# Decode attention with a gated MLP on one core: the last projection chunks in two column tiles and two PSUM tiles, a one-chunk last load, and bias loads on SyncE's queue

## The chip, the core and the metric

The kernel runs on one core of one Trainium2 chip. The metric is the device time of one execution in microseconds; the median of several runs is given. Beside it stands one profiled execution, whose trace all views come from. TensorE is PE (its weight loads PEld), VectorE is DVE, ScalarE is ACT, GpSimd is POOL, SyncE is SP. All times are in microseconds from the start of the span unless another unit is named.

## The reference

Eight tokens (batch 8, one position each) of width 448 go through two branches, which a gate mixes.

```python
g = sigmoid((x * gate_w).sum(-1))
# A: attention of one query over the last W = 1024 positions of a cache
q = (x @ wq)                                  # 16 heads of 256, 8 key/value heads
scores = einsum("bhqd,bhkd->bhqk", q, k) * 256 ** -0.5
a = einsum("bhqk,bhkd->bhqd", softmax(scores), v).reshape(8, 1, 4096) @ wo
# B: layernorm, then an MLP with 1792 hidden units
b = gelu(layernorm(x) @ w1 + b1) @ w2 + b2
out = g * a + (1 - g) * b                     # 8 x 448
```

All tensors are bf16. For every token the kernel reads 4 MiB of keys and 4 MiB of values; with the weights that is 77.67 MB.

## The kernel before

**Loads.** All large loads go through a ring of four slots (`slot`, 4 MiB each) in the order of a plan: keys 0, wq, keys 1, values 0, keys 2, values 1, and so on to values 6, then w1 (with room for w2), values 7 with w2, and wo. They are all issued by SP (`nc.sync.dma_start`: L128 for keys and values, L140 for rows of weights, L157 for w2). A slot is loaded again once what read it is done (`done()`, `pump()`). Keys and values of a token are cut in two halves by key/value heads (`kv_loader`); `cuts` cuts the halves again: keys 0 has `(2, 1)`, its first half in two pieces of 1024 KB and its second half in one of 2048 KB. In the built program each transfer counts its landing on one of eight counters, taken in turn, and its issue waits for the landing of the transfer eight before it.

**Each token.** `transpose_keys(b)` turns the keys on TensorE (L360) and copies them out on ACT (L366) and DVE (L368); one group of sixteen goes by DVE and POOL (L330, L338). `scores(b)` multiplies with the queries (L427), `top` takes the maximum (L440), `expo` the exponential (L444), `turn`, `scale` and `bring` make the weights ready for `values(b)` (L498), and `finish` and `spread` (L511 to L524) put the sums of heads into `oP`, which is the stationary operand of the last projection. The order of all this is written out by hand; `steps(b)` places the softmax of one token between the transposes of the next.

**Biases.** `biases` issues the loads of b2 (one row) and b1 (four rows of 448, on partitions 0, 32, 64, 96) on ACT's queue, after the transposes of token 1 (`steps(0)`, place 15). `norm`, in the transposes of token 2 (place 14), spreads these rows over partitions on DVE (L307, L309) before the reduction of token 2's scores (L440).

**The last projection.** What is left at the end is 46 chunks, each a product of an 8-column stationary operand with 128 rows of 448 columns: 14 of the MLP (`hs` with w2), 32 of the attention (`oP` with wo). The wo load is cut by `cuts` into pieces of whole chunks, eight chunks to each of four quarters `q`: quarters 0 and 1 in one piece each, quarter 2 in two pieces of 4, quarter 3 in pieces of 2, 4 and 2 chunks. The first 40 chunks are `wide` (L632): chunk i goes to column tile i % 4 of TensorE and so to a 32-partition block of the PSUM tile A1. DVE adds b2 to A1 (`accs`, L639). The last `TAIL` = 6 chunks are `narrow` (L643): each is cut in four column blocks of 112, one per column tile, all in one PSUM tile A2. Between them, at place `TAIL - LATE` = 4, stands the product with `pick` (f32, L643), which adds up the four blocks of `accs`. Then DVE copies blocks 0 and 1 of A2 and ACT blocks 2 and 3 (L656), and each half is stored by SP and by ACT (L657).

Of the kernel before, what the change touches and what calls it, by code (L numbers as in the profile page):

```python
# [11 lines left out]
BF16 = mybir.dt.bfloat16  # L12
F32 = mybir.dt.float32
# [4 lines left out]
def kernel(  # L18
# [15 lines left out]
    nc = tc.nc  # L34
    P = nc.NUM_PARTITIONS

    NB, Sq, D = A_x.shape
# [8 lines left out]
    QD = 4  # L46
    BL = P // QD
# [13 lines left out]
    NCK = W // SK  # L61
    CB = 4
    UR = NG * rep
    HALF = D // 2
    DO = D // QD
    J8 = Dh // BL
    NQW = Hq // QD
    HS = NCK * Dh
    SLOT = NG * HS
    RING = 4  # L70
    TAIL = 6
    LATE = 2
    qscale = float(Dh) ** -0.5

    xf = A_x.rearrange("b s d -> (b s) d")
    out_f = out.rearrange("b s d -> (b s) d")

    ctx.enter_context(tc.manual_schedule())
    consts = ctx.enter_context(tc.tile_pool(name="consts", bufs=1))
# [6 lines left out]
    ps_kt = ctx.enter_context(tc.tile_pool(name="ps_kt", bufs=3, space=PSUM))  # L86
# [19 lines left out]
    def add(key, loader):  # L106
        index[key] = len(plan)
        plan.append(loader)

    def slot(*key):  # L110
        return slots[index[key]]

    def kv_loader(src, b, cuts=(1, 1), inner=False):
        pieces = [
            (i, k, cuts[i])
            for i in range(NG)
            for k in range(cuts[i])
        ]
        if inner:
            pieces.sort(key=lambda x: x[1])  # L120

        def load(t):
            for i, k, m in pieces:
                v = src[b, i * QD : (i + 1) * QD, kv_base:Sk, :].rearrange(
                    "a (s c) d -> s a (c d)", c=NCK
                )
                n = HS // m
                nc.sync.dma_start(  # L128
                    t[:, i * HS + k * n : i * HS + (k + 1) * n],
                    v[:, :, k * n : (k + 1) * n],  # L130
                )

        return load

    def rows_loader(pieces):
        def load(t):
            o = 0
            for ap in pieces:
                n = ap.shape[-1]
                nc.sync.dma_start(t[:, o : o + n], ap)  # L140
                o += n

        return load
# [12 lines left out]
        kv_loader(A_v_cache, NB - 1, (2, 2), True)(t)  # L156
        nc.sync.dma_start(slot("w12")[:, OW2 : OW2 + FB * D], w2_v)  # L157

    add(("k", 0), kv_loader(A_k_cache, 0, (2, 1)))
    add(("wq",), rows_loader(wq_r + [wq_t]))  # L160
    for b in range(1, NB):
        add(("k", b), kv_loader(A_k_cache, b))
# [4 lines left out]
        (NQW - 2, 0, 4),  # L167
        (NQW - 2, 4, 8),
        (NQW - 1, 0, 2),
        (NQW - 1, 2, 6),  # L170
        (NQW - 1, 6, 8),
    ]
    add(("wo",), rows_loader([wo_v[:, q, j0 * D : j1 * D] for q, j0, j1 in cuts]))

# [4 lines left out]
    b2_r = consts.tile([BL, D], BF16)  # L179
    b1_r = consts.tile([P, FQ], BF16)  # L180
# [1 line left out]
    nc.scalar.dma_start(g_r[0:1, :], gate_w.rearrange("(o d) -> o d", o=1))  # L182

    def biases():
        nc.scalar.dma_start(b2_r[0:1, :], B_b2.rearrange("(o d) -> o d", o=1))
        nc.scalar.dma_start(b1_r[::BL, :], B_b1.rearrange("(t d) -> t d", t=QD))

    ident = consts.tile([P, P], BF16)
    make_identity(nc, ident[:])
# [418 lines left out]
    b = NB - 1  # L608
# [10 lines left out]
    finish(b)  # L619
    spread(b)  # L620

    A2 = ps_kt.tile([P, DO], F32, tag="ktp", name="A2")
    w2 = slot("w12")
    w = slot("wo")
    NCH = NQW * J8
# [2 lines left out]
    ] + [(oP[:, c % J8, c // J8, :], w[:, c * D : (c + 1) * D]) for c in range(NCH)]  # L628
    wide, narrow = chunks[:-TAIL], chunks[-TAIL:]
    for i, (lhsT, rhs) in enumerate(wide):  # L630
# [4 lines left out]
            rhs=rhs,  # L635
# [3 lines left out]
    nc.vector.tensor_tensor(accs[:], A1[:], b2s[:], op=ALU.add)  # L639
    narrow.insert(TAIL - LATE, (pick[:], accs[:]))  # L640
    for i, (lhsT, rhs) in enumerate(narrow):
        for t in range(QD):
            nc.tensor.matmul(  # L643
                A2[BL * t : BL * t + NB, :],
                lhsT=lhsT,
                rhs=rhs[:, t * DO : (t + 1) * DO],
                start=(i == 0),
                stop=(i == TAIL),
            )
    for h, (eng, copy) in enumerate(  # L650
        ((nc.sync, nc.vector.tensor_copy), (nc.scalar, nc.scalar.copy))
    ):
        res = consts.tile([NB, 2, DO], BF16, name=f"res{h}")
        for i in range(2):
            t = 2 * h + i
            copy(res[:, i, :], A2[BL * t : BL * t + NB, :])  # L656
        eng.dma_start(  # L657
            out_f[:, h * HALF : (h + 1) * HALF], res[:].rearrange("b i d -> b (i d)")
        )


# [28 lines left out]
```

## Time and profile before

| what | value |
|---|---|
| median of 3 runs | 193.32 us (193.28 to 193.37) |
| the profiled execution | 193.19 us, span 191.4 us |
| mean granted TensorE clock | 0.854 |
| busy share: PE, DVE, ACT, POOL | 62%, 57%, 48%, 29% |
| SP's DMA queue | 77.67 MB, 96.3% of 16 engines' span |
| last matmul of L643 starts its group | 187.21 us |
| last store issued (ACT) | 188.82 us |

The span runs from the first instruction of the program to the last; the execution's own time has 1.8 us more around it. A line of the timeline gives start, duration, engine, line and operation, operands with shapes, and in brackets the idle time before it and what ended that. In the table by stage each row is one stretch of time: busy time of each engine with the number of instructions in brackets, then the granted clock as a share, the share of time that the DMA engines were busy, and GB/s. The chain of waits is the work that ended last, followed back from the end: at each step the start, the length and what it was.

### The profile page before, as it was taken

The page shows a single profiled execution, that of the slowest core. Times are in us where ns is not written, and L with a number is a line of the kernel's source. Part 1 is how long each engine was busy: PE and PEld are TensorE (multiplying, and loading weights), DVE is VectorE, ACT ScalarE, POOL GpSimd, SP SyncE. Part 2 cuts the span into 40 slices and gives each one's busy share as a digit, 9 for nine tenths or more (in the row PEclk, how much of TensorE's full clock was granted, in tenths as well). Part 3 has the DMA queues.
Part 4 walks back from the last instruction along what each step waited for, and adds up shares of the span by engine and source line. Part 5 has one row for each costly group of instructions (what it writes and reads, how often), then busy time and mean ns, then how long its engine had stood idle before and what let it go on. Part 6 is the DMA issues. An engine that isn't in the chain of part 4 may idle for free.

```text
span 191.4 us, 2916 instructions
## 1 busy us (share of the span) xinstructions
PE 119.1 (62%) x1114; PEld 77.0 (40%) x1114; DVE 108.7 (57%) x248; ACT 91.9 (48%) x105; POOL 55.4 (29%) x143
## 2 busy tenths in 40 slices
PE   0658509679784397738773676669854885083552
PEld 0646104555671185317641563168514761010111
DVE  4284673964889467705870687037822885847311
ACT  2298420894992259525852594228822892000001
POOL 8480000570750066005700480049002910000000
PEclk9999855999999969996999999756997999855555
DMA  5999999999999999999999999999999999999980
GB/s 204 445 402 425 440 435 419 425 421 432 422 430 428 428 421 431 426 431 428 418 431 425 421 435 428 428 428 416 431 431 428 425 425 420 403 422 430 407 321 3
DMA packets 7129, 77.86 MB, mean 407 GB/s; under 512 B 830, under 2 KB 1228, under 8 KB 1996
## 3 DMA queue, kind: packets, MB, share of 16 engines
q1 hardware_dynamic: 7072, 77.67, 96.3%
q8 instruction: 8, 0.13, 0.3%
q14 instruction: 5, 0.04, 0.1%
q10 hardware_dynamic: 44, 0.02, 0.0%
HBM read 77.67 MB, written 0.01 MB: 406 GB/s over the span
## 4 chain that ended last, share of the span: by engine, by line
DMA 73%; PE 10%; DVE 7%; ACT 4%; SPq 2%; issue 2%; DVEq 0%; ACTq 0%
DMA slot<-in_A_k_cache_dram 42%; DMA slot<-in_A_v_cache_dram 14%; DMA slot<-in_A_wq_dram 9%; DMA slot<-in_A_wo_dram 8%; PE ktp L360 7%; ACT kt L366 3%; DVE kt L368 2%; PE S_ps L427 2%; DVE qw L419 1%; SPq L128 1%; SPq L140 1%; DVE EZ L462 1%; PE S_ps L391 1%; DVE qt L404 1%; DVE nmx L440 1%
## 5 line engine op out<-in xcount | busy, mean ns | idle before, releaser
L366 ACT COPY kt<-ktp 128x1024 bf16<-128x1024 bf16 x80 | 76.1, 1024 | 37.0 <-PE ktp L360 36.9
L360 PE MATMUL ktp<-ident_f,slot 128*128 128x128 f32 x480 | 71.7, 305 | 31.4 <-DMA slot<-in_A_k_cache_dram 22.9
L360 PEld LDWEIGHTS ktp<-ident_f,slot 128*128 128x128 f32 x480 | 60.2, 157 | 49.2 <-issue 23.6
L338 POOL COPY kt<-B 32x128 f32<-32x128 f32 x128 | 51.3, 401 | 97.8 <-DVE B L330 86.3
L368 DVE COPY kt<-ktp 128x1024 bf16<-128x1024 bf16 x40 | 27.5, 689 | 16.9 <-PE ktp L360 16.5
L498 PE MATMUL PO<-slot,ET 128*16 128x512 bf16 x256 | 18.1, 429 | 16.2 <-DMA slot<-in_A_v_cache_dram 16.2
L444 ACT ACTIVATE E<-S_ps,nmx 128x1024 f32<-128x1024 f32 x8 | 8.9, 1114 | 28.7 <-DVE nmx L440 28.7
L330 DVE STREAM_TRANSPOSE B<-slot 128x512 f32<-128x512 f32 x8 | 5.7, 711 | 29.7 <-DMA slot<-in_A_k_cache_dram 29.6
L427 PE MATMUL S_ps<-kt,qw 128*4 128x512 bf16 x256 | 17.9, 419 | 5.4 <-DVE qw L419 5.4
L498 PEld LDWEIGHTS <-ET 128*16 128x16 bf16 x256 | 6.1, 94 | 27.6 <-DMA slot<-in_A_v_cache_dram 21.0
L440 DVE TENSOR_REDUCE nmx<-S_ps 128x1 f32<-128x1024 f32 x8 | 9.8, 1222 | 10.0 <-PE S_ps L427 10.0
L427 PEld LDWEIGHTS <-qw 128*4 128x4 bf16 x256 | 6.6, 85 | 14.0 <-DVE qw L419 6.5
L451 DVE STREAM_TRANSPOSE EB<-E 128x1056 f32<-128x1056 f32 x8 | 10.2, 1271 | 1.3 <-ACT E L444 1.3
L524 DVE TENSOR_TENSOR oP<-Y 32x32 bf16<-32x32 f32 x32 | 9.4, 295 | 1.1
L656 ACT CAST res<-A 8x112 bf16<-8x112 f32 x2 | 0.5, 246 | 15.8 <-DVE res L656 15.8
L481 DVE TENSOR_TENSOR ET<-sm,mask 128x512 bf16<-128x512 f32 x8 | 5.5, 692 | 2.2 <-PE sm L473 2.1
L511 DVE STREAM_TRANSPOSE T<-PO 128x512 f32<-128x512 f32 x8 | 5.7, 709 | 1.0 <-PE PO L498 0.9
L566 ACT ACTIVATE zb<-za 128x448 f32<-128x448 f32 x1 | 0.6, 577 | 10.8 <-DVE za L565 10.8
L473 PE MATMUL sm<-EZ,perm 128*128 128x128 bf16 x8 | 1.7, 216 | 6.0 <-DVE EZ L462 5.9
L632 PE MATMUL A<-slot,oP 128*8 128x448 bf16 x26 | 3.5, 547 | 2.5 <-DMA slot<-in_A_wo_dram 2.5
L639 DVE TENSOR_TENSOR accs<-A,b2s 128x448 f32<-128x448 f32 x1 | 0.6, 624 | 7.1 <-PE A L632 7.1
L516 DVE TENSOR_TENSOR Y<-T 64x64 f32<-64x64 f32 x16 | 4.0, 248 | 0.5
(91 smaller groups left out, 58.1 us busy)
## 6 DMA issues: line engine op xcount, KB each, us to landing
slot<-in_A_k_cache_dram SPq DMA_DIRECT2D x15, 2048.0 KB, 28.1
slot<-in_A_v_cache_dram SPq DMA_DIRECT2D x14, 2048.0 KB, 30.2
slot<-in_A_v_cache_dram SPq DMA_DIRECT2D x4, 1024.0 KB, 23.9
slot<-in_A_wq_dram SPq DMA_DIRECT2D x3, 1024.0 KB, 17.1
slot<-in_A_k_cache_dram SPq DMA_DIRECT2D x2, 1024.0 KB, 6.4
slot<-in_A_wo_dram SPq DMA_DIRECT2D x2, 896.0 KB, 18.7
slot<-in_B_w_dram SPq DMA_DIRECT2D x1, 1568.0 KB
slot<-in_B_w_dram SPq DMA_DIRECT2D x1, 1344.0 KB, 26.4
```

What stands on the lines that cost most here:

```text
L330: nc.vector.transpose(B[:].rearrange("p c w s a -> p (c w s a)"), kn[:, c0 * P : (c0 + CB) * P],)
L338: nc.gpsimd.tensor_copy(words[BL * w : BL * (w + 1), :, c0 : c0 + CB, g * S8 : (g + 1) * S8, 0], B[BL * g : BL * (g + 1), :, w].rearrange( ...
L360: nc.tensor.transpose(words[:, c, :, 0], kn[:, o : o + P], ident_f[:])
L366: nc.scalar.copy(dst, src)
L368: nc.vector.tensor_copy(dst, src)
L427: nc.tensor.matmul(S_ps[BL * t : BL * t + UR, n * QN : (n + 1) * QN], lhsT=qw[:, j, b, t, rep * u : rep * u + UR], rhs=KT[u][:, t, n * CQ ...
L440: nc.vector.reduce_max(nmx[:], S_ps[:], axis=AXIS.X, negate=True)
L444: nc.scalar.activation(E[:, 0:W], S_ps[:], ACT.Exp, bias=soft.pop(b)[:], scale=1.0, accum_out=E[:, W : W + 1],)
L451: nc.vector.transpose(EB[:].rearrange("p c r -> p (c r)"), E[:])
L498: nc.tensor.matmul(PO[BL * t : BL * t + Hq], lhsT=ET[:, c].rearrange("p u a r -> p (u a r)"), rhs=vn[:, c], start=(c < QD), stop=(c >= NCK ...
L511: nc.vector.transpose(T[:], PO[:].rearrange("p u (e j) -> p u j e", j=J8))
L524: nc.vector.tensor_tensor(oP[BL * i : BL * (i + 1), :, :, b], Yv[0:BL, :, :, i], Yv[BL : 2 * BL, :, :, i], op=ALU.add,)
```

## The change

Four things are changed:

- `TAIL` goes from 6 to 8 and `LATE` from 2 to 1: eight narrow chunks instead of six, and `pick` stands before the last one instead of the last two.
- A narrow chunk is cut in two blocks of 224 columns instead of four of 112, in column tiles 0 and 1; each block has a PSUM tile of its own. One copy per half takes it out, DVE's and ACT's, and each half has its own store as before.
- The last quarter of wo is loaded in pieces of 2, 3, 2 and 1 chunks instead of 2, 4 and 2; the second half of keys 0 in two pieces instead of one.
- The biases are loaded by SP's queue, b1 in two transfers of two rows instead of one of four.

```diff
-    HALF = D // 2
-    DO = D // QD
+    DO = D // 2
...
-    TAIL = 6
-    LATE = 2
+    TAIL = 8
+    LATE = 1
...
-    add(("k", 0), kv_loader(A_k_cache, 0, (2, 1)))
+    add(("k", 0), kv_loader(A_k_cache, 0, (2, 2)))
...
         (NQW - 1, 0, 2),
-        (NQW - 1, 2, 6),
-        (NQW - 1, 6, 8),
+        (NQW - 1, 2, 5),
+        (NQW - 1, 5, 7),
+        (NQW - 1, 7, 8),
...
     def biases():
-        nc.scalar.dma_start(b2_r[0:1, :], B_b2.rearrange("(o d) -> o d", o=1))
-        nc.scalar.dma_start(b1_r[::BL, :], B_b1.rearrange("(t d) -> t d", t=QD))
+        nc.sync.dma_start(b2_r[0:1, :], B_b2.rearrange("(o d) -> o d", o=1))
+        for t in range(0, QD, 2):
+            nc.sync.dma_start(
+                b1_r[BL * t : BL * (t + 2) : BL, :],
+                B_b1.rearrange("(t d) -> t d", t=QD)[t : t + 2, :],
+            )
...
-    A2 = ps_kt.tile([P, DO], F32, tag="ktp", name="A2")
+    A2 = [ps_kt.tile([P, DO], F32, tag="ktp", name="A2") for h in range(2)]
...
     for i, (lhsT, rhs) in enumerate(narrow):
-        for t in range(QD):
+        for h in range(2):
             nc.tensor.matmul(
-                A2[BL * t : BL * t + NB, :],
+                A2[h][BL * h : BL * h + NB, :],
                 lhsT=lhsT,
-                rhs=rhs[:, t * DO : (t + 1) * DO],
+                rhs=rhs[:, h * DO : (h + 1) * DO],
                 start=(i == 0),
                 stop=(i == TAIL),
             )
...
-        res = consts.tile([NB, 2, DO], BF16, name=f"res{h}")
-        for i in range(2):
-            t = 2 * h + i
-            copy(res[:, i, :], A2[BL * t : BL * t + NB, :])
-        eng.dma_start(
-            out_f[:, h * HALF : (h + 1) * HALF], res[:].rearrange("b i d -> b (i d)")
-        )
+        res = consts.tile([NB, DO], BF16, name=f"res{h}")
+        copy(res[:], A2[h][BL * h : BL * h + NB, :])
+        eng.dma_start(out_f[:, h * DO : (h + 1) * DO], res[:])
```

In the changed kernel the lines named above stand four further down (the narrow matmuls at L647, the copies at L658, the stores at L659).

## The prediction

> **What bounds the kernel now.** I read the page first: its slices, its queues and its chain. The loads run without a gap from the first slice to the last but one, all on SyncE's queue, and the chain is 73% DMA.
>
> ```profile
> PEclk9999855999999969996999999756997999855555
> DMA  5999999999999999999999999999999999999980
> q1 hardware_dynamic: 7072, 77.67, 96.3%
> DMA 73%; PE 10%; DVE 7%; ACT 4%; SPq 2%; issue 2%; DVEq 0%; ACTq 0%
> ```
>
> So the time is the load stream (77.67 MB whatever the kernel does) plus what follows the last load. An edit counts if it makes the stream longer, lets it run dry, or changes that tail. Next I read the end of the chain of waits in order of time, and the timeline of the same stretch.
>
> ```profile
> 171.89 14.57 DMA slot<-in_A_wo_dram
> 186.46 0.04 issue
> 186.51 1.15 PE A L643 x31
> 187.65 0.25 DVE res L656
> 187.91 0.31 DVEq L685
> ...
> 188.55 0.25 ACT res L656
> ```
>
> ```profile
> 186.51 0.54 PE L643 MATMUL A<-slot,oP 128*8 128x112 bf16 x16 [0.56 <-DMA slot<-in_A_wo_dram]
> 186.83 0.59 PE L643 MATMUL A<-accs,pick 128*8 128x112 f32 x8
> 187.21 0.40 PE L643 MATMUL A<-slot,oP 128*8 128x112 bf16 x8
> 187.64 0.56 DVE L656 CAST res<-A 8x112 bf16<-8x112 f32 x2 [1.03 <-PE A L643]
> 188.23 0.36 SPq L657 DMA_DIRECT2D out_dram<-res  x1
> 188.29 0.50 ACT L656 CAST res<-A 8x112 bf16<-8x112 f32 x2 [15.77 <-DVE res L656]
> 188.82 0.31 ACTq L657 DMA_DIRECT2D out_dram<-res  x1
> ```
>
> The reader should see a tail in series: matmuls, two DVE copies, then two ACT copies that wait for DVE (both read the one tile A2), then ACT's store. By the trace's landing records the last three wo pieces land at 185.37, 186.46 and 187.03, the SP store at 189.46 and the ACT store at 190.05, each 1.23 after its issue began. The span ends 1.36 after that. The table by stage gives the granted clock there:
>
> ```profile
> 149.24:166.31 17.07, 10.30 (x113) 6.43 (x112) 13.36 (x33) 9.36 (x11) 4.25 (x11) 1.00 1.00 419
> 166.31:180.30 13.99, 7.54 (x60) 1.70 (x60) 8.13 (x18) 0.58 (x1) 0.00 (x0) 0.50 1.01 421
> 186.50:187.65 1.15, 1.10 (x32) 0.76 (x31) 0.12 (x2) 0.00 (x0) 0.00 (x0) 0.50 0.00 0
> ```
>
> The columns are busy times of PE, PEld, DVE, ACT and POOL, then clock, DMA share and GB/s: the tail's matmuls run at half clock.
>
> **The change, part by part.** The profiled execution took 193.19, span 191.4, so 1.8 lies around the span; the median of the runs is 193.32, 0.13 above it. I work out a difference in the profiled execution and add it to the median.
>
> *Load stream, +0.14.* Packet records give the price of shorter rows: a 16384 B packet takes a median of 613 ns (mean 616), 8192 B 312 (318), 3584 B 144, 1792 B 74. The second half of keys 0 was 8 packets of 16384 B on each of the 16 DMA engines and becomes 16 of 8192 B: 16 x 312 - 8 x 613 = 88 ns, and a 9 ns completion packet for the extra piece: +0.10 (by the means +0.16). The last quarter of wo was cut 2, 4, 2 chunks and becomes 2, 3, 2, 1. Along the line through 1792 and 3584, 896 B takes 39 ns and 2688 B 109: before 8 x (74 + 144 + 74) + 27, after 8 x (74 + 109 + 74 + 39) + 36, so +0.04. The Trainium skill (DMA: Bandwidth & Descriptors, Specifications) puts line rate at 512 B and more, by which both terms would be nothing; the rows disagree, since 1792 B at 74 ns is 387 GB/s over 16 engines and 16384 B at 613 ns is 428. Bounds 0 and +0.25, the latter with the three bias rows on the slowest engine.
>
> *TensorE tail, +0.65.* A narrow matmul of 112 columns starts 0.093 after the one before it in its column tile (186.559, 186.646, 186.739), a pass of the f32 pick matmul 0.187 after (186.83, 187.02, 187.21), and there are two passes. From its last start a matmul needs 0.298, of which 0.093 is streaming. Four column tiles run side by side. Now two do, each twice as wide: 0.187 a chunk, 2 x 0.374 = 0.748 for pick. With 8 narrow chunks and LATE 1, the q=3 pieces feed chunks 0-1, 2-4, 5-6 and 7; pick stands behind chunk 6, in order, ahead of chunk 7. The wide chunks end at about 185.37 (the four after 184.83 at 0.53), so accs (0.624) is ready at 186.03 and no longer decides. Chunks 2-4 (3 x 0.187) end about when the next piece lands, so the path starts from that landing, which stands one 896 B piece (0.31 to 0.33) ahead of the last. From it: 0.04 wake, chunks 5-6 0.374, pick 0.748, chunk 7 0.187, drain 0.205, sum 1.55; from the last landing 1.55 - 0.32 = 1.23. Before it was 187.61 - 187.03 = 0.58. So +0.65. The new last piece is small, but pick, which was half as long, now covers it.
>
> *Copies and issue, -0.77.* Before, ACT's store was issued 188.82 - 187.61 = 1.21 after the last matmul. After, DVE and ACT each copy 8x224 from a tile of their own; the built program has the ACT copy wait for TensorE alone. No row has 8x224. For DVE, 112 columns take 264 ns and 448 (L639) 624, so 224 take 385; for ACT 246 and 577 (L566), so 356. These lie between the rows for 112 and 448; I take the line. Last matmul to issue: 0.03 + 0.385 + 0.03 = 0.44 on SP, the same within 0.02 on ACT. 0.44 - 1.21 = -0.77. Bounds -0.95 (a copy as short as for 112) and -0.55 (as long as for 448).
>
> *Two stores at once, +0.10.* Before, the issues were 0.59 apart. After they coincide. The nearest rows: L177 on ACT's queue beside L128 on SP's took 0.58 and its first packet came 0.95 after its start (a store's alone: 0.79); L182 beside another load took 0.24 and L185 0.23, undisturbed; L186 took 0.61. From below nothing, from above 0.30 + 0.16; I take 0.10, nearest to the undisturbed small ones.
>
> *End, +0.06.* SP waits for all counters at the end. The two stores now stand ahead of two more such waits instead of one (0.065 each, from 188.65 and 188.72). One wait of before, behind the last landing, took 0.44 for no reason that the trace shows; if that falls ahead of the landing, 0.37 is won.
>
> *Edits costed at nothing.* Biases: ACT loses two issues (0.23 and 0.61 at 44.2), but waits for DVE until 47.46 anyway. On SP the three issues (about 0.3 to 0.6 each) stand behind value loads of batch 1 and ahead of keys 3. Every transfer takes one of eight completion counters in turn and waits for the landing of the one eight before: the biases then hold three, and the second half of keys 3 waits until 47.7 (was 44.77), the values 2 until about 52 (48.77). At 47.7 four loads of 2 MB are still in flight, 20 us at 420 GB/s: the stream doesn't run dry. The rows land behind the values of batch 1, at about 62.4 (ACT's landed by 48.9, overtaking). L307 needs them at 61.63: DVE stalls up to 0.9, and the reduction at 63.18 with it. Cover: the next keys land only at 67.32, 3 after DVE is free; beyond that cover each us would stall TensorE's transposes. The earlier transposes of keys 0 (from 13.75 to about 11.2) end in the wait for wq until 22.40. The extra issue at the start (0.58) delays only loads that queue behind 4 MB.
>
> Sum: 0.14 + 0.65 - 0.77 + 0.10 + 0.06 = +0.18, so 193.32 + 0.18 = 193.50, within 0.2% (0.39, about what a measurement of this kernel can tell from no change: 192.93 to 193.71). What is late next, once the copies run side by side, is pick's f32 passes.
>
> **Rivals.**
> Faster: TensorE gets full clock in the tail. Then the streaming of 1.31 halves, -0.65: 192.85. For it: the stage up to 166.31 had 1.00 with PE busy 60% of it. Against: from 166.31 on 0.50 with 54%, and the change gives PE fewer matmuls there. The Trainium skill (TensorE: Matmul & The Clock Gate, Part 1) says that a busy window of 3.4 us brings the full clock and an idle one takes it away; the trace's steps are multiples of 3.41, but its busy stage at 0.50 shows no such return. Chance 0.06.
> Slower: the two stores disturb each other. Place: the two issues that now coincide; price 0.30 in the issue (0.61 against 0.31) and 0.16 to the first packet, 0.46 in place of 0.10: 193.86. It decides from 0.31 on. For it: L177 and L186 beside SP's issues; against: L182 and L185. Chance 0.20.
> Slower: the biases come late. If they land over 3 after 61.6, batch 3 starts late and the ring's next loads with it; it costs the time only once 20 us of loads in flight are used up, and then what is over: 194 at 1 us. Chance 0.05.
> That the copies still wait on each other (+0.36, 193.86) speaks against the built order: 0.02.
>
> **How the numbers follow.** The forecast has 0.67; its own range, with copies, stream and end wait at their bounds, is 193.05 to 193.75, with 0.06 of it below 192.93 and 0.06 above 193.71. Faster 0.06 + 0.06 = 0.12; slower 0.20 + 0.05 + 0.02 + 0.06 = 0.33; within 0.55. The range reaches to the faster rival and past the slower ones: 192.85 to 194.1.
>
> **What would show it.** Right: last wo landing about 0.14 later; last narrow matmul 1.2 after it; the pick matmuls behind a wait for wo, not for accs; DVE and ACT copies starting within 0.05 of each other, both about 0.37; both stores issued at one time, 0.45 behind the last matmul; L307 behind a wait for b_r near 62. Wrong: a clock of 1.00 in the last stage, a dip in the DMA slices before the end, store issues of 0.6, or chunk spacings other than 0.187.

## The result and the profile after

The changed kernel takes 193.06 us (median of 22 runs, 192.93 to 193.18) against 193.31 of the kernel before (22 runs, 193.15 to 194.36): ratio 0.9981, 95% interval 0.9973 to 0.9989. So it is a little faster, by 0.25, where 0.18 slower was forecast. Between the two profiled executions the difference is 0.09 (193.10 against 193.19); the other 0.16 is that the profiled execution of before stood 0.12 below the median of its runs, and that of after 0.04 above.

First the slices of the page and its main queue, after. The load stream is as full as before.

```profile
DMA  5999999999999999999999999999999999999980
q1 hardware_dynamic: 7370, 77.67, 96.5%
```

The end of the chain of waits, after (start, length, what):

```profile
172.03 14.29 DMA slot<-in_A_wo_dram
186.32 0.04 issue
186.36 2.11 PE A L647 x16
188.47 0.37 DVE res L658
```

The chain leaves the loads at 186.32, with the piece of chunks 2 to 4, because TensorE is never idle behind it in this view: 2.11 of TensorE, where before it was 1.15 from 186.46. The starts of the single matmuls say more. Chunk 4 starts at 186.686, so at 0.187 a chunk the next would start at 186.873. Chunk 5 starts at 186.961, 0.04 behind the landing of its own piece at 186.919. So it is that landing, 0.29 ahead of the last (187.21), from which TensorE runs without another wait, as the prediction had it. The timeline of that stretch:

```profile
185.55 0.54 PE L647 MATMUL A<-slot,oP 128*8 128x224 bf16 x4
186.36 1.14 PE L647 MATMUL A<-slot,oP 128*8 128x224 bf16 x10 [0.27 <-DMA slot<-in_A_wo_dram]
187.29 0.96 PE L647 MATMUL A<-accs,pick 128*8 128x224 f32 x4
188.03 0.40 PE L647 MATMUL A<-slot,oP 128*8 128x224 bf16 x2
188.46 0.38 DVE L658 CAST res<-A 8x224 bf16<-8x224 f32 x1 [2.27 <-PE A L647]
188.50 0.34 ACT L658 CAST res<-A 8x224 bf16<-8x224 f32 x1 [15.85 <-PE A L647]
188.86 0.30 ACTq L659 DMA_DIRECT2D out_dram<-res  x1
188.87 0.32 SPq L659 DMA_DIRECT2D out_dram<-res  x1
```

Pick's four matmuls stream 0.75 (187.29 to 188.03) and stand ahead of the last chunk, which had landed at 187.21. The two copies run side by side and both stores are issued at once. The tail's clock in the table by stage (PE, PEld, DVE, ACT, POOL, clock, DMA share, GB/s) is half, as before:

```profile
185.50:188.43 2.93, 2.63 (x24) 1.09 (x19) 0.62 (x1) 0.00 (x0) 0.00 (x0) 0.50 0.19 69
```

Step by step, by the traces' records (landing records for loads and stores):

| step | before | after | change | forecast |
|---|---|---|---|---|
| last wo landing | 187.03 | 187.21 | +0.18 | +0.14 |
| to the end of the last matmul | 0.58 | 1.22 | +0.64 | +0.65 |
| to the issue of the later store | 1.21 | 0.44 | -0.77 | -0.77 |
| to the landing of the later store | 1.23 | 1.43 | +0.20 | +0.10 |
| to the end of the span | 1.35 | 1.02 | -0.33 | +0.06 |

Four steps came out within 0.1. The last one, after all data had landed, turned a loss of 0.25 into a gain of 0.08.

### The profile page after: what moved, and what is told of

Same layout as the page of the kernel before. It is cut to its first block, busy times and chain, and to the rows that moved or that the text cites. A ratio compares the mean times of both kernels' runs of the same rounds, so it can differ in the third digit from the quotient of the medians.

```text
span 191.3 us, 2889 instructions
## 1 busy us (share of the span) xinstructions
PE 121.7 (64%) x1100; PEld 78.9 (41%) x1100; DVE 108.5 (57%) x247; ACT 92.5 (48%) x104; POOL 55.6 (29%) x143
## 4 chain that ended last, share of the span: by engine, by line
DMA 75%; PE 10%; DVE 7%; ACT 4%; issue 1%; ACTq 0%; DVEq 0%
DMA slot<-in_A_k_cache_dram 45%; DMA slot<-in_A_v_cache_dram 14%; DMA slot<-in_A_wq_dram 8%; DMA slot<-in_A_wo_dram 7%; PE ktp L364 6%; ACT kt L370 3%; DVE kt L372 2%; PE S_ps L431 2%; DVE qw L423 1%; PE A L647 1%; DVE EZ L466 1%; DVE qt L408 1%; DVE nmx L444 1%; DVE EB L455 1%; DVE sc L464 1%
## 5 line engine op out<-in xcount | busy, mean ns | idle before, releaser
L364 PE MATMUL ktp<-ident_f,slot 128*128 128x128 f32 x480 | 72.8, 307 | 29.7 <-DMA slot<-in_A_k_cache_dram 20.1
L364 PEld LDWEIGHTS ktp<-ident_f,slot 128*128 128x128 f32 x480 | 61.1, 158 | 48.4 <-issue 22.4
L502 PE MATMUL PO<-slot,ET 128*16 128x512 bf16 x256 | 18.8, 441 | 17.6 <-DMA slot<-in_A_v_cache_dram 17.6
L502 PEld LDWEIGHTS <-ET 128*16 128x16 bf16 x256 | 6.9, 96 | 28.5 <-DMA slot<-in_A_v_cache_dram 13.5
L658 ACT CAST res<-A 8x224 bf16<-8x224 f32 x1 | 0.3, 337 | 15.8 <-PE A L647 15.8
L636 PE MATMUL A<-slot,oP 128*8 128x448 bf16 x24 | 2.9, 549 | 2.5 <-DMA slot<-in_A_wo_dram 2.5
```

The source lines that it names most:

```text
L364: nc.tensor.transpose(words[:, c, :, 0], kn[:, o : o + P], ident_f[:])
L502: nc.tensor.matmul(PO[BL * t : BL * t + Hq], lhsT=ET[:, c].rearrange("p u a r -> p (u a r)"), rhs=vn[:, c], start=(c < QD), stop=(c >= NCK ...
```

## The experiments

**What happens behind the last landing.** At the end SP waits, one instruction after the other, for the counters of loads, stores and engines. When nothing is outstanding, such instructions start 0.06 to 0.07 apart, with 0.04 to 0.06 between the end of one and the start of the next. In both traces one such gap was 0.44 to 0.45, and it stood ahead of instruction 81 of SP's list, counted from 0 in the built program (79 in the trace, which leaves out two branches). The records of SP, each with its start:

| instruction | before | after |
|---|---|---|
| ahead of 81 | wait for ACT's store, 190.07 to 190.10 | issue of SP's store, 188.87 to 189.19 |
| 81 | last wait, **190.54** | first wait, **189.64** |
| 82 | drain (DRAIN in the trace), 190.63 | wait for SP's store, 189.72 to 190.32 |
| 83 | drain, 190.71 | wait for ACT's store, 190.36 |
| 84, 85 | | two waits for loads, 190.42 and 190.49 |

Before, the stop (190.10 to 190.54) fell behind the last landing at 190.05. After, five transfers more stood ahead (one piece of keys 0, one of wo, three of biases), and the stop (189.19 to 189.64) fell where the stores were still under way to 190.30.

Theory 1 is that SP always stops for 0.44 at that place of its list, and that the change's SP instructions have moved another instruction onto it. Theory 2 is that the biases on ACT's queue had slowed or disturbed the load stream. Theory 3 is that the tail itself brings the gain. Four kernels separate them. Each kernel's ratio is the one on record (not that of the medians), to runs of the kernel before on the same chip (medians 193.32 to 193.36; 193.31 beside the changed kernel's 193.06). Where a kernel is compared with the changed kernel or with another experiment, the two may come from different chips, and the kernel before differed between them by up to 0.05.

**e1_keys0_cut**: the kernel before with one more SP instruction, a load cut in two, and nothing else.

```diff
-    add(("k", 0), kv_loader(A_k_cache, 0, (2, 1)))
+    add(("k", 0), kv_loader(A_k_cache, 0, (2, 2)))
```

> The kernel before with one edit: the second half of keys 0 in two pieces, so one more transfer and one more instruction of SP. Theory 1 (a stop at a fixed place of SP's instruction list): in both traces SP loses 0.44 to 0.45 us ahead of the same instruction, number 81 of its list counted from 0; before that is the last wait, behind the last store's landing; after it is the first wait, ahead of the landing. Here one more instruction moves number 81 onto the wait for SP's own store, which lands later than the stop ends: the stop is hidden. Expected 0.47 less from the last landing to the end of the span (1.36 to 0.89), 0.10 more for shorter rows in the stream: 192.95 against 193.31. Theory 2 (biases on ACT's queue slow the stream): 193.4. Theory 3 (the narrow chunks, copies and stores bring it): 193.4.

Measured 192.99 (ratio 0.9981, 0.9965 to 0.9998). The last wo landing was 0.12 later, from the last store's landing to the end it took 0.86 (before 1.35). A cut that only lengthens the stream made the kernel as fast as the whole change does. Theories 2 and 3 can't explain that: neither the biases nor the tail is touched.

**e3_tail_only**: the whole new tail, with as many SP transfers as before. Against the changed kernel:

```diff
-    add(("k", 0), kv_loader(A_k_cache, 0, (2, 2)))
+    add(("k", 0), kv_loader(A_k_cache, 0, (2, 1)))
...
-    cuts = [(q, 0, J8) for q in range(NQW - 2)] + [
-        (NQW - 2, 0, 4),
-        (NQW - 2, 4, 8),
+    cuts = [(q, 0, J8) for q in range(NQW - 1)] + [
...
-        nc.sync.dma_start(b2_r[0:1, :], B_b2.rearrange("(o d) -> o d", o=1))
-        for t in range(0, QD, 2):
-            nc.sync.dma_start(
-                b1_r[BL * t : BL * (t + 2) : BL, :],
-                B_b1.rearrange("(t d) -> t d", t=QD)[t : t + 2, :],
-            )
+        nc.scalar.dma_start(b2_r[0:1, :], B_b2.rearrange("(o d) -> o d", o=1))
+        nc.scalar.dma_start(b1_r[::BL, :], B_b1.rearrange("(t d) -> t d", t=QD))
```

> The changed kernel's tail alone: eight narrow chunks in two tiles, LATE 1, copies, stores and the pieces 2, 3, 2, 1; keys 0 and the biases as before, and quarter 2 of wo in one piece, so that SP issues as many transfers as before. Theory 1: number 81 of SP's list is the drain behind both stores' waits, so the stop of 0.44 stays behind the last landing; the tail itself is last landing to last matmul 1.22 (was 0.58), to the store's issue 0.43 (was 1.21), to its landing up to 1.43 (was 1.23): 193.35 to 193.45 against 193.31. Theory 2: 193.3. Theory 3 (the tail brings the gain): 193.05.

Measured 193.38 (0.9997, 0.9983 to 1.001): no gain. The stop stood at the drain behind all waits (190.30 to 190.75), and the last landing to the end took 1.44.

**e4_after_biases_act**: the changed kernel with the biases back on ACT's queue, three SP instructions fewer.

```diff
-        nc.sync.dma_start(b2_r[0:1, :], B_b2.rearrange("(o d) -> o d", o=1))
-        for t in range(0, QD, 2):
-            nc.sync.dma_start(
-                b1_r[BL * t : BL * (t + 2) : BL, :],
-                B_b1.rearrange("(t d) -> t d", t=QD)[t : t + 2, :],
-            )
+        nc.scalar.dma_start(b2_r[0:1, :], B_b2.rearrange("(o d) -> o d", o=1))
+        nc.scalar.dma_start(b1_r[::BL, :], B_b1.rearrange("(t d) -> t d", t=QD))
```

> The changed kernel with the biases back on ACT's queue as before, so three SP instructions fewer. Theory 1: number 81 of SP's list is the wait behind the two that wait for the stores, so the stop of 0.44 stands behind the last landing again: 0.3 to 0.4 slower than the changed kernel (193.06), 193.4. Theory 2 (biases on ACT's queue slow the stream): also slower, but with the last wo landing later by that much and no gap of 0.4 in SP's waits at the end. Theory 3 (tail): 193.05.

Measured 193.50 (1.0006, 0.9997 to 1.0014), 0.44 slower than the changed kernel, with the last wo landing at the same time (187.20) and the stop at 190.33 to 190.76, behind the stores' landing at 190.30. Theory 2 would have had the landing later.

**e2_biases_sp**: the kernel before with the biases on SP's queue, three SP instructions more.

```diff
-        nc.scalar.dma_start(b2_r[0:1, :], B_b2.rearrange("(o d) -> o d", o=1))
-        nc.scalar.dma_start(b1_r[::BL, :], B_b1.rearrange("(t d) -> t d", t=QD))
+        nc.sync.dma_start(b2_r[0:1, :], B_b2.rearrange("(o d) -> o d", o=1))
+        for t in range(0, QD, 2):
+            nc.sync.dma_start(
+                b1_r[BL * t : BL * (t + 2) : BL, :],
+                B_b1.rearrange("(t d) -> t d", t=QD)[t : t + 2, :],
+            )
```

> The kernel before with one edit: b1 and b2 by SP's queue, three more instructions of SP. Theory 1 (stop at number 81 of SP's list): 81 is now the third wait of the end, ahead of both landings, so hidden: 0.47 less behind the last landing, stream the same within 0.05: 192.85 to 192.95 against 193.31. Theory 2 (biases on ACT's queue slow the stream and spread the runs of before): last landing earlier by 0.2 or more and the runs within 0.3 of each other, 193.05. Theory 3 (tail): 193.3.

Measured 193.91 (1.0026, 1.0016 to 1.0036): slower by 0.6 where all theories had it level or faster. The stop was where theory 1 puts it (188.65 to 189.10, ahead of both landings), and from the last landing to the end it took 0.85. But ACT's store, issued at 188.78, landed 2.39 later in place of 1.23. The DMA view of e2_biases_sp from 188.9 to 190.9 (forty slices of 0.05, then queues: packets, MB, share) shows what came between:

```profile
DMA  0120000000000110700000000000000000000000
...
q14 instruction: 1, 0.01, 1.9%
```

The first 1 and 2 are SP's store, the pair of 1s near 189.55 to 189.65 ACT's store, and the 7 at 189.70 a packet of 8192 B on the instruction queue, which took 0.62 by the packet records (189.73 to 190.35). The same view of before has no such packet:

```profile
DMA  0012000000000011000000000000000000000000
```

Seven of the eight rows of ACT's store left by 189.63; the eighth at 190.35, as that packet ended. In before that packet came at 191.17, when all was over. One follows every stop whose end can be read, 0.63 to 0.66 behind that end (0.90 in the changed kernel). Of the 1.16 by which ACT's store landed later, the row's delay is 0.72; what took the rest is not shown.

**e10_biases_two_transfers** tells whether it was that packet or the biases: the same move with one SP instruction less.

```diff
-        nc.scalar.dma_start(b2_r[0:1, :], B_b2.rearrange("(o d) -> o d", o=1))
-        nc.scalar.dma_start(b1_r[::BL, :], B_b1.rearrange("(t d) -> t d", t=QD))
+        nc.sync.dma_start(b2_r[0:1, :], B_b2.rearrange("(o d) -> o d", o=1))
+        nc.sync.dma_start(b1_r[::BL, :], B_b1.rearrange("(t d) -> t d", t=QD))
```

> The kernel before with the biases on SP's queue in two transfers (b2, and b1's four rows in one): one SP instruction less than e2_biases_sp. If e2_biases_sp lost its time because the 8192 B instruction packet that follows SP's stop by 0.63 met the ACT store's row on one DMA engine, it doesn't here: the stop falls one wait later, from about 188.81 to 189.26, the packet comes at 189.9 or later, the store's rows leave at 189.57 to 189.70 as before, and the stop is hidden ahead of the SP store's landing: 192.85 to 192.95 against 193.33. If it is the biases on SP's queue that cost e2_biases_sp its 0.6: 193.7 to 193.9.

Measured 192.93 (0.9988, 0.9972 to 1.0005, an interval that reaches just past no change; four of the twelve runs took 193.16 to 194.01, with spans of 191.0 to 191.2 like the others), 0.98 faster than with the biases in three transfers. The same DMA view of e10_biases_two_transfers:

```profile
DMA  0000001200000000001100004000000000000000
...
q14 instruction: 1, 0.01, 1.1%
```

ACT's store is at 189.80 to 189.90, and the instruction packet (the 4 at 190.10) comes behind it. So theory 1 holds, with an addition: the stop of 0.44, about 0.4 more than an ordinary step, is paid if it falls behind the last landing and hidden if it falls ahead, and the packet that follows can cost more if it meets a store. That the packet held the row is read from the times alone.

The place of the stop in some of the kernels (SP's instruction 81; times from the traces):

| kernel | 81 is | stop | last store landed | from there to the end |
|---|---|---|---|---|
| before | last wait | 190.10 to 190.54 | 190.05 | 1.35 |
| after | first wait | 189.19 to 189.64 | 190.30 | 1.02 |
| e1_keys0_cut | wait for SP's store | within the wait to 189.62 | 190.20 | 0.86 |
| e2_biases_sp | third wait | 188.65 to 189.10 | 191.17 | 0.85 |
| e3_tail_only | drain | 190.30 to 190.75 | 190.19 | 1.44 |
| e4_after_biases_act | wait behind that for SP's store | 190.33 to 190.76 | 190.30 | 1.39 |
| e10_biases_two_transfers | wait for SP's store | within the wait to 189.71 | 190.29 | 0.92 |

**What the spans add.** Each run has its span beside its time. The time around the span was 1.73 to 1.85 in all 22 runs of the changed kernel, but 1.74 to 3.31 in the 77 runs of the kernel before that stand beside the experiments, over 1.85 in 42 of them. By means, the span is 191.46 before and 191.28 after (single spans are on record to 0.1). So of the 0.25 some 0.18 was won in the span and the rest around it. No kernel with two column tiles went over 1.85, whether the biases were on ACT's queue (e3_tail_only, e4_after_biases_act) or not; of those with four, e1_keys0_cut, e2_biases_sp, e6_four_tiles and e10_biases_two_transfers had runs of 2.1 to 2.9, e8_four_tiles_early_pick, with six runs, at most 1.88. As far as these runs tell, that part goes with the two tiles, and its cause is open. It does not touch theory 1: by the mean spans e1_keys0_cut wins 0.36 (191.08 against 191.45 on its chip), and e3_tail_only loses 0.15 (191.60).

**What the tail costs.** The tail's terms came out as forecast, but one trace of a sum doesn't show which part holds the path, so each was changed by itself, from the changed kernel.

**e5_pick_bf16**: one bf16 pass for pick in place of two f32 ones.

```diff
-    accs = consts.tile([P, D], F32)
+    accs = consts.tile([P, D], BF16)
...
-    pick = consts.tile([P, NB], F32)
+    pick = consts.tile([P, NB], BF16)
...
```

> The changed kernel with accs and pick in bf16 (so the sums of the wide chunks are rounded to bf16 ahead of the last addition): pick is one pass of 0.187 us for 224 columns in place of two of 0.374. If the f32 passes behind chunk 6 hold the path, as the prediction had it, the last matmul ends 0.56 earlier behind the same landing and the time is 192.50 against 193.06 of the changed kernel. If the path is elsewhere (the end of SP, the stores alone), 193.0.

Measured 192.53 (0.9954, 0.9938 to 0.9971), 0.53 less than the changed kernel; the last matmul ended 0.69 behind the last landing (1.22).

**e6_four_tiles**: narrow chunks in four column tiles of 112 again, two per PSUM tile, and two copies of 112 on each engine.

```diff
...
-        for h in range(2):
+        for t in range(QD):
...
-                A2[h][BL * h : BL * h + NB, :],
+                A2[t // 2][BL * t : BL * t + NB, :],
...
```

> The changed kernel with each narrow chunk again in four column tiles of 112 columns, two in each of the two PSUM tiles, and two copies of 112 on DVE and on ACT, side by side. TensorE from the landing of the piece before the last: 0.04 + 2 x 0.093 + 0.374 (pick) + 0.093 + 0.205, so 0.61 less than now; the copies 0.56 in place of 0.38, 0.18 more: 192.63 against 193.06. If the width of the tiles doesn't matter (TensorE not on the path): 193.25, by the longer copies.

Measured 192.78 (0.9973, 0.9959 to 0.9986), 0.28 less where 0.43 was expected. The tail's parts were right: last landing to last matmul 0.58 (0.64 less), to the issue 0.61 (0.17 more). But in this execution the last wo piece landed at 187.36, 0.15 later than in the changed kernel, whose loads are the same; what moves that landing by 0.1 to 0.3 from one execution to another wasn't looked into. This execution took 192.96, 0.18 above the median, so its landing does not explain the median; by the mean spans the edit wins 0.36, and a part of the shortfall lies around the span.

**e7_after_keys0_uncut**: keys 0 cut as before, one SP instruction less.

```diff
-    add(("k", 0), kv_loader(A_k_cache, 0, (2, 2)))
+    add(("k", 0), kv_loader(A_k_cache, 0, (2, 1)))
```

> The changed kernel with keys 0 cut as before: rows of 16384 B in the second half, one SP instruction less. The stream is 0.10 shorter by the packet records; number 81 of SP's list becomes the wait for ACT's store, which lands after the stop has ended, so the stop stays hidden: 192.96 against 193.06. If the place of the stop was not what the cut changed and the cut itself helps: 193.2 or more.

Measured 192.91 (0.9971, 0.9961 to 0.9981), 0.15 less; the last landing was at 187.04 (187.21). The stop stayed ahead of the landing (189.10 to 189.54, at the second wait, which is for loads, not at the wait for ACT's store as expected). So the cut costs about what the packet records say (0.10 to 0.16), and helps only where, as in e1_keys0_cut, it moves the stop.

**e11_after_pick_early**: pick ahead of chunk 2.

```diff
-    LATE = 1
+    LATE = 6
```

> The changed kernel with pick ahead of chunk 2 (LATE 6) and nothing else. TensorE's work behind accs (ready at 186.19) is then in one piece: pick 0.748, chunks 2 to 7 at 0.187 each: last start 187.91 in place of 188.03, so 0.12 less: 192.94 against 193.06. If the order is what matters rather than the length of the f32 passes, 0.75 less: 192.35.

Measured 192.92 (0.9974, 0.9964 to 0.9985), 0.14 less. With two tiles and f32 it is the amount of streaming that binds, not the place of pick.

**e8_four_tiles_early_pick** and **e9_two_tiles_bf16_early** put the parts together; both have keys 0 uncut and LATE 6, the first the edit of e6_four_tiles, the second that of e5_pick_bf16.

> The version that the reading points to: the changed kernel with keys 0 uncut, four column tiles in two PSUM tiles, and pick ahead of chunk 2 (LATE 6), in the time in which TensorE waits for the next piece. The last matmul then ends 0.04 + 0.093 + 0.205 = 0.34 behind the last landing (now 1.22), the copies cost 0.18 more, the stream is 0.10 shorter: 193.06 - 0.88 + 0.18 - 0.10 = 192.26.

> The changed kernel with two column tiles kept, accs and pick in bf16 (rounded as in e5_pick_bf16), pick ahead of chunk 2 (LATE 6) and keys 0 uncut. From e5_pick_bf16 (192.53): chunk 7 no longer behind pick's 0.187, of which 0.03 comes back ahead of chunk 2, and 0.13 for keys 0: 192.24, level with four tiles (192.33), since one copy of 224 is 0.16 shorter than two of 112 and the narrow chunks are that much longer.

Measured 192.33 (0.9941, 0.9925 to 0.9956) and 192.21 (0.9942, 0.993 to 0.9953): both beat both kernels. The timeline of e8_four_tiles_early_pick:

```profile
185.61 0.62 DVE L644 TENSOR_TENSOR accs<-A,b2s 128x448 f32<-128x448 f32 x1 [6.58 <-PE A L637]
186.29 0.56 PE L648 MATMUL A<-accs,pick 128*8 128x112 f32 x8 [0.35 <-DVE accs L644]
186.62 0.93 PE L648 MATMUL A<-slot,oP 128*8 128x112 bf16 x24
187.58 0.54 DVE L661 CAST res<-A 8x112 bf16<-8x112 f32 x2 [1.35 <-PE A L648]
```

Here pick waits for accs, not for a load, and runs while the piece of chunks 2 to 4 is landing (186.35); the last matmul ends 0.31 behind the last landing (187.24), which is one wake, one chunk and the drain. What is left on the path is the copy, the store and the end. In e9_two_tiles_bf16_early the last matmul ends 0.53 behind its landing and the single copies win most of that back:

```profile
186.28 1.33 PE L648 MATMUL A<-slot,oP 128*8 128x224 bf16 x12
187.65 0.38 DVE L659 CAST res<-A 8x224 bf16<-8x224 f32 x1 [1.56 <-PE A L648]
188.06 0.32 SPq L660 DMA_DIRECT2D out_dram<-res  x1
```

## Why the prediction was wrong

- **The step that failed is "End, +0.06".** It measured -0.33. The sum counted the waits behind the last landing and left the one of 0.44 where it was, "for no reason that the trace shows". Its possible gain of 0.37 was named and then given no place in the sum and no rival of its own; with it End would have been -0.31 and the sum 193.13, where 193.06 was measured. e1_keys0_cut, e3_tail_only and e4_after_biases_act show the reason: a fixed place of SP's list, which the change's additional SP instructions shift. Had the gap been taken as bound to a place of the list rather than to its wait, the two built programs would have told that the change moves it ahead of the stores' landing.
- **The way from trace to median, taken as fixed: 0.17 off.** The forecast added the difference of the profiled executions to the median of before, which stood 0.13 above its profile. The median of after lies 0.04 below its own. In part the profiled spans were not typical (191.41 and 191.32, where the means are 191.46 and 191.28), in part the time around the span scatters before and not after. This is the smaller part of the 0.44 by which 193.50 was missed; End is 0.39, and the other steps take back 0.13.
- **Load stream, +0.14: right by the packets, not clear of noise by the landing.** The last landing was 0.18 later; e7_after_keys0_uncut wins back 0.15 by uncutting keys 0 and e1_keys0_cut lands 0.12 later by cutting it. But the landings are from single executions, and four traces with the same loads (the changed kernel, e5_pick_bf16, e6_four_tiles, e11_after_pick_early) have that landing anywhere from 187.06 to 187.36. The new rows measured 108 ns for 2688 B and 41 ns for 896 B (forecast 109 and 39). The 512 B that the Trainium skill (DMA: Bandwidth & Descriptors, Specifications) gives as the least transfer for line rate, by which the term would have been nothing, doesn't fit these rows: 896 B at 41 ns is 350 GB/s over 16 engines, 16384 B at 613 ns 428.
- **TensorE tail, +0.65: right,** 0.64, and by the path that was forecast, from the landing one piece ahead of the last. Chunk starts 0.187 apart where TensorE doesn't wait, pick's passes 0.374 (187.286, 187.659, 188.033). e5_pick_bf16 and e6_four_tiles confirm both factors by 0.53 and 0.64 of tail.
- **Copies and issue, -0.77: right.** The copies took 378 ns on DVE and 337 on ACT (forecast 385 and 356) and started 0.03 apart. The copies no longer wait on each other, as the built order said.
- **Two stores at once, +0.10: too small,** 0.20. SP's store landed 1.43 behind its issue, ACT's 1.25; why only SP's is slower is not shown. The rival's mechanism did not appear: the issues took 0.30 and 0.32, no longer than before. From the later issue to the later landing it took 1.42 to 1.44 in every kernel in which both stores are issued at once, and 1.23 to 1.25 where one goes after the other (e2_biases_sp apart).
- **Biases: right to cost nothing by themselves.** SP issued them at 27.0, 33.3 and 38.2; the second half of keys 3 went out at 47.94 (forecast 47.7), the values 2 at 52.88 (52). L311 (L307 before) started at 61.94, about 0.15 behind the copy ahead of it (a stall of up to 0.9 was allowed for), and the reduction at 63.49 (63.18 before), while the next keys' transposes waited until 67.60 anyway. Their effect was on SP's list, not on the queue or on DVE.
- **Full clock in the tail: no.** The clock was 0.50 from 173.72 to the end. That it had been 1.00 from 170.30 to 173.72 fits the clock gate of the Trainium skill (TensorE: Matmul & The Clock Gate, Part 1), which a busy window of about 3.4 us opens: the stretch before, 166.89 to 170.30, had PE busy 2.85 of 3.41.

In the traces the whole is small because two of the tail's terms, of 0.6 and 0.8, nearly cancel; a third of 0.33 decided the sign. That the load stream came out within 0.04 of its forecast is in part luck, since the landing moves by up to 0.3 between executions.

## What to carry to other kernels

Count the end of the span like any other stage: behind the last landing, go through every instruction of the engine that closes the program, and ask of each gap whether it belongs to an instruction or to a place in the list; a transfer added far ahead can move it. When a last reduction is cut into fewer, wider tiles so that its result leaves in one copy, the price is in what streams per tile, f32 passes doubly; put such a pass where the engine waits for data anyway, or make it one pass. Price the parts of a change by single edits before believing that the change as a whole is worth its small gain: here the cut of keys 0 cost 0.15, the wider tiles 0.64 of the tail against 0.17 won in the copies, and the version without them and with pick moved wins 1.0 in place of 0.25.

## What the runs showed of the hardware

- SP stopped for 0.44 to 0.46 at instruction 81 of its list in every trace in which the end of the stop can be read, whatever stood there: a wait that was already met, or a drain. A packet of 8192 B on the instruction queue follows, 0.63 to 0.66 behind the stop's end (0.90 in the changed kernel). That the stop is the crossing into the next block of instructions is inferred from that packet. The Trainium skill (Runtime: NRT & Kernel Launch, Instruction fetch mechanics) has engines fetch their instructions in blocks over a DMA queue of their own, at a cost that is mostly hidden. If the stop is such a crossing, it is hidden here only where a wait covers it.
- One row of a store went 0.7 behind the other seven, as such a packet ended, and the store landed 1.2 later (e2_biases_sp).
- Two stores of eight rows, issued by SP and ACT within 0.01, landed 1.42 to 1.44 behind the later issue, against 1.23 to 1.25 where one goes after the other; the issues took no longer (0.30 and 0.32).
